# Token rows of u by VectorE block transposes and transfers inside SBUF instead of TensorE transposes, in a fused attention and Fourier-mixing kernel

## The chip, the cores and the metric

The kernel runs on one core of one Trainium2 chip. The metric is the device time of one execution in microseconds (us), the median of several runs. A core has a matrix engine (TensorE, PE), a vector engine (VectorE, DVE), a scalar engine (ScalarE, ACT), GpSimd (POOL) and a queue engine (SyncE, SP) that here only issues transfers (DMAs). Each engine works through its own list of instructions in order; an instruction that waits holds up all that stand behind it on its engine.

## The reference, cut to what matters

Four batches of 768 tokens. Attention with 8 heads of 64 channels gives x (768 tokens by 512 channels) of each batch. Then a Fourier mixing layer and a two-layer perceptron:

```python
X = np.fft.fft(np.fft.fft(x, axis=1), axis=2)
u = x + np.real(X)
mu = np.mean(u, axis=-1, keepdims=True)
var = np.mean((u - mu) ** 2, axis=-1, keepdims=True)
un = (u - mu) / np.sqrt(var + 1e-06)
out = u + np.maximum(un @ w_ch1, 0.0) @ w_ch2     # w_ch1 (512, 2048), w_ch2 (2048, 512)
```

So u is needed twice: with channels on the partitions, as the right operand of the product with w_ch1, and with tokens on the partitions, for the statistics of a token and for the sum with the result.

## The kernel before

All is in fp32. The attention of batch b runs interleaved with the mixing and the perceptron (`mix`, `mlp7`) of batch b-1; those of batch 3 run alone at the end. Within the bulk of the program a scheduler orders the instructions of each engine by its own model of durations, and a tile framework gives out buffers and sets the waits; the code gives the work, not its exact order.

Attention, per pair of heads n and block of keys c (`weigh`, `values`, `scale`): scores (L869), exponentials on ScalarE (L873), a mask by VectorE (L879), VectorE's running sum of the weights (L964), the product with v (L890). When a pair is done its sums are turned and inverted: L908 on TensorE, L915, L917, L918 and L925 on VectorE, eight small copies L924 on ScalarE, and L929 scales x.

`mix` adds the Fourier transform to x in place, in four blocks of 128 channels (matmuls L1091, sums L1105). After it x holds u turned: channel on the partition, token along the row, as x[:, c, token] with c from 0 to 3.

`mlp7` multiplies by blocks in Strassen's manner (Winograd's form): seven products instead of eight. The left operands are blocks of w_ch1 and sums of them (A11, A12, A22, S1 to S4), written to DRAM (`ad`) in batch 0 and fetched from there into a ring of NR = 12 buffers, one for each product (L1339, on SP; a fetch waits until the product that last used its buffer is done). The right operands are the quarters b11, b12, b21, b22 of x and the sums t1, t2, t4 (L1344 to L1346) and t3 (L1351); t3 is written over b12. So whatever reads the first two channel blocks of tokens 384 to 767 must have read them before t3 is written.

For each of 16 row blocks (two halves of eight, index f) the loop `inner` makes seven products of two matmuls of 128x384 each (L1366), in four PSUM banks' worth of names p1, p6, p5, p7, which come from a pool of two banks while attention runs beside it. ScalarE copies each result out of PSUM, which frees the bank, VectorE adds (L1392, L1399, L1404, L1408, L1416) and ScalarE applies relu; four pieces of `hall` result. `outer7` then makes the second layer from `hall`, one half after the other (L1246).

`across(b, T, u)` makes token rows: for one of six blocks T of 128 tokens, four TensorE transposes of 128x128 (L1117) into PSUM and one ScalarE copy of 128x512 into the buffer of T (L1118). For T = 3, 4, 5 it runs before t3 is written, for T = 0, 1, 2 in the first row block of `inner` (in batch 0, after the first half). Four of the six buffers (`us`) lie in the memory of w_ch1, which is free after batch 0; two come from a pool. `spread` takes the statistics of each T from them (L1123, L1125, then POOL) when `outer7` begins on the first half; the last sums add the result to the same rows and `store` sends them out.

The memory of w_ch1 is cut up by hand: the ring, the sums t1, t2, t4, the rows `us`, two side buffers.

Of the kernel before, what the change touches and what calls it, by code (L numbers as in the profile page):

```python
# [11 lines left out]
F32 = mybir.dt.float32  # L12
# [8 lines left out]
P = 128  # L21
B, H, S, D = 4, 8, 768, 64
NBITS = 6
DM = H * D
DFF = 4 * DM
NT = S // P
# [4 lines left out]
NDC = DM // P  # L31
GTT = 2
GT = GTT * P
# [446 lines left out]
def _main(  # L480
# [13 lines left out]
    nc = tc.nc  # L494
# [13 lines left out]
    def wt(shape, dtype, tag, name, bufs=2):  # L508
        return work.tile(shape, dtype, tag=tag, name=name, bufs=bufs)
# [4 lines left out]
    def pt(shape, name):  # L514

        turn[0] += 1
        if roomy[0] and turn[0] % 2:
            if turn[0] % 4 == 1:
                return ps_o.tile(shape, F32, tag="o", name=name)
            return ps_sc.tile(shape, F32, tag="sc", name=name)  # L520
        return ps_1.tile(shape, F32, tag="ps", name=name)
# [468 lines left out]
    GT = NT // 2  # L990
# [54 lines left out]
    def mix(b):  # L1045
# [39 lines left out]
        for j in range(NDC):  # L1085
# [22 lines left out]
            yield  # L1108

        yield from mlp7(b)  # L1110

    def across(b, T, u):

        x = xs[b]
        ps = pt([P, NDC, P], f"un{b}_{T}")
        for c in range(NDC):
            nc.tensor.transpose(ps[:, c, :], x[:, c, T * P : (T + 1) * P], ident)  # L1117
        nc.scalar.copy(u, ps.rearrange("p c n -> p (c n)"))  # L1118

    def spread(b, T, u):  # L1120
# [14 lines left out]
    HF = NFC // 2  # L1135
    A11, A12, A22, S2, S1, S3, S4 = range(7)
    ad = tc.dram_tile([HF, 7, P, 2, P], F32, name="ad")
    w1f = w1.rearrange("p c f -> p (c f)")
    NR = 12
    ring = [  # L1140
        w1f[:, i * 2 * P : (i + 1) * 2 * P].rearrange("p (k m) -> p k m", k=2)
        for i in range(NR)
    ]
    at = NR * 2 * P
    bs = [
# [1 line left out]
        for i in range(3)  # L1147
    ]
    at += 3 * S
    us = [w1f[:, at + i * DM : at + (i + 1) * DM] for i in range(4)]  # L1150
    at += 4 * DM
    side = [w1f[:, at + i * HALF : at + (i + 1) * HALF] for i in range(2)]
    HD = DM // 2
    tq = wt([P, 6, HD], F32, "tq", "tq", 1)
# [154 lines left out]
    def mlp7(b):  # L1309
        x = xs[b]  # L1310
# [5 lines left out]
        ut, sd, ss = [*us], side, s1s  # L1316
        if b == 0:
# [9 lines left out]
            ut = spare[0:3] + [s1s[1].rearrange("p r n -> p (r n)")]  # L1327
# [8 lines left out]
        def fetch():  # L1336
            n = fetched[0]
            if b and n < len(todo):
                nc.sync.dma_start(ring[n % NR], ad[todo[n][0], todo[n][1]])  # L1339
                fetched[0] += 1  # L1340

        for _ in range(NR):
            fetch()
        nc.vector.tensor_tensor(t1, b12, b11, op=ALU.subtract)  # L1344
        nc.vector.tensor_tensor(t2, b22, t1, op=ALU.subtract)
        nc.vector.tensor_tensor(t4, b21, t2, op=ALU.subtract)  # L1346
        ut += [wt([P, DM], F32, "u", f"u{b}_{T}", 2) for T in range(4, NT)]
        for T in (3, 4, 5):
            across(b, T, ut[T])
        rs = {}  # L1350
        nc.vector.tensor_tensor(t3, b22, b12, op=ALU.subtract)  # L1351
        hall = wt([P, 2, HF // 2, S], F32, "F", f"h{b}", 1)
        done = [0]

        def product(i, ps, start=True):
            n = done[0]
            left = ring[n % NR]
            if b == 0:
# [14 lines left out]
        def inner(half):  # L1373
            for r in range(HF // 2):
                f = half * HF // 2 + r
                c11, c12, c21, c22 = (
                    hall[:, i, r, g * HALF : (g + 1) * HALF]
                    for i in range(2) for g in range(2)
                )

                def bank(nm):
                    return pt([P, HALF], f"h{b}_{f}_{nm}")

                p1 = bank("p1")
                product(A11, p1)
                nc.scalar.copy(c12, p1)  # L1388
                p6 = bank("p6")
                product(S2, p6)  # L1390
                nc.scalar.copy(c21, p6)  # L1391
                nc.vector.tensor_tensor(c21, c12, c21, op=ALU.add)  # L1392
                yield
                product(A12, p1, False)
                nc.scalar.activation(c11, p1, AF.Relu)
                p5 = bank("p5")
                product(S1, p5)
                nc.scalar.copy(c22, p5)  # L1398
                nc.vector.tensor_tensor(c22, c21, c22, op=ALU.add)  # L1399
                yield  # L1400
                p7 = bank("p7")
                product(S3, p7)
                nc.scalar.copy(sd[0], p7)  # L1403
                nc.vector.tensor_tensor(c22, c22, sd[0], op=ALU.add)  # L1404
                nc.scalar.activation(c22, c22, AF.Relu)
                product(S4, p5, False)
                nc.scalar.copy(c12, p5)
                nc.vector.tensor_tensor(c12, c21, c12, op=ALU.add)  # L1408
                nc.scalar.activation(c12, c12, AF.Relu)
                if b and f == 0:  # L1410
                    for T in range(3):
                        across(b, T, ut[T])
                yield
                product(A22, p7, False)
                nc.scalar.copy(sd[1], p7)
                nc.vector.tensor_tensor(c21, c21, sd[1], op=ALU.add)  # L1416
                nc.scalar.activation(c21, c21, AF.Relu)
                if b == 0 and r < HF // 2 - 1:
                    quarters(f + 1)
                if r % 2:  # L1420
                    yield
# [148 lines left out]
```

## Time and profile before

| | |
|---|---|
| time, three runs (us) | 1104.84, 1107.59, 1108.07; median 1107.59 |
| the profiled execution (us) | 1106.46; its span from first to last instruction 1104.7 |
| TensorE clock granted | 0.991 of full |
| transfers | 175567 packets, 103.13 MB, mean 93 GB/s |

The profile is one execution, taken by the hardware profiler. A group line gives the source line, the engine, the operation, "output <- inputs" by the program's names, the shapes and the count, then the busy time and the mean of one in ns, then the idle time of that engine just ahead of these instructions and what ended it. The chain of waits goes back from the last instruction, at each step to what released it. A timeline line gives start and length in us; a bracket is the engine's idle time before it and what ended it. Starts of TensorE's matmuls overlap, so the distance between starts is what one costs.

### The profile page before, as it was taken

To read this page: it belongs to the slowest core of one execution; us is meant where nothing else is said; L and a number is where in the kernel's file an instruction comes from. 1 tells how busy PE (TensorE), PEld (TensorE's weight loads), DVE (VectorE), ACT (ScalarE), POOL (GpSimd) and SP (SyncE) were. 2 spreads that over 40 slices of the span, in tenths; PEclk is the share of its full clock that TensorE was granted. 3 is DMA by queue.
4 is the path that set the end of the run, shared out by engine and by line. 5 is a ranking of instruction groups with operands and counts; after the bars stand their busy time and mean duration, and the time that the engine had idled before them with its cause. 6 is when DMAs were issued, how large, how long until landed. Compare 5 with 4: busy or idle time off the path is not lost.

```text
span 1104.7 us, 14065 instructions
## 1 busy us (share of the span) xinstructions
PE 1050.9 (95%) x4893; PEld 636.6 (58%) x4893; DVE 790.0 (72%) x1326; ACT 500.3 (45%) x1055; POOL 63.1 (6%) x141
## 2 busy tenths in 40 slices
PE   6989888999989999999999999999999999999996
PEld 3334354445744675545664576645674569768575
DVE  5779968979598977786758785975856785644353
ACT  5869556654267324354426424354315532340420
POOL 0000000002000020010000011001000002100000
PEclk9989999999999999999999999999999999999998
DMA  8744534261046262313144134213032205122301
GB/s 225 201 99 96 101 106 109 99 196 26 20 130 183 73 192 52 63 58 76 26 152 110 49 67 167 44 38 91 20 109 85 69 26 172 53 82 91 119 20 42
DMA packets 175567, 103.13 MB, mean 93 GB/s; under 512 B 129408, under 2 KB 162816, under 8 KB 175488
## 3 DMA queue, kind: packets, MB, share of 16 engines
q1 hardware_dynamic: 168400, 83.93, 28.8%
q0 software_dynamic: 5520, 17.83, 5.2%
q8 instruction: 41, 0.67, 0.2%
q10 hardware_dynamic: 1568, 0.39, 0.2%
q14 instruction: 38, 0.31, 0.1%
HBM read 81.14 MB, written 20.97 MB: 92 GB/s over the span
## 4 chain that ended last, share of the span: by engine, by line
PE 56%; DVE 8%; ACT 3%; issue 1%; DMA 1%; DVEq 0%; ACTq 0%
PE o L1246 20%; PE h_p L1366 19%; PE oo L890 6%; PE sc L869 5%; PE cs L1062 2%; DVE pk L879 2%; PE A L1091 2%; PE B L1091 1%; DVE acc L964 1%; ACT rr L924 1%; DMA zraw<-in_moe_w_ch_dram 1%; PE un L1117 1%; DVE w L1258 1%; PE bits L804 1%; DVE h L1232 1%
## 5 line engine op out<-in xcount | busy, mean ns | idle before, releaser
L1246 PE MATMUL o<-w,h 128*128 128x256 f32 x1152 | 259.4, 382 | 1.1 <-ACT tq L1265 0.7
L1246 PEld LDWEIGHTS o<-w,h 128*128 128x128 f32 x1152 | 216.3, 190 | 43.5 <-issue 4.6
L873 ACT ACTIVATE pk<-sc 128x768 f32<-128x768 f32 x192 | 148.0, 808 | 82.4 <-PE sc L869 63.9
L1366 PE MATMUL h_p<-x,w 128*128 128x384 f32 x448 | 163.1, 494 | 3.6 <-ACT h L1388 2.3
L890 PE MATMUL oo<-pk,vn 128*64 128x385 f32 (+1 forms) x768 | 156.9, 503 | 3.6 <-DVE pk L879 3.0
L869 PE MATMUL sc<-qt,kt 64*128 64x384 f32 x768 | 155.3, 507 | 3.3 <-ACT pk L873 3.0
L879 DVE SCALAR_TENSOR_TENSOR pk<-qb,kb,pk 128x768 f32<-128x768 bf16 x132 | 128.9, 1012 | 29.1 <-ACT pk L873 28.9
L1366 PEld LDWEIGHTS h_p<-x,w 128*128 128x128 f32 x448 | 82.0, 190 | 71.0 <-ACT pk L873 5.4
L964 DVE TENSOR_TENSOR acc<-acc,pk 128x1536 f32<-128x1536 f32 (+1 forms) x72 | 105.7, 1482 | 6.6 <-ACT pk L873 6.1
L1366 PE MATMUL h_p<-w 128*128 128x384 f32 x288 | 105.5, 489 | 2.2 <-ACT w L1403 2.2
L890 PEld LDWEIGHTS oo<-pk,vn 128*64 128x64 f32 x768 | 49.7, 137 | 98.6 <-issue 71.8
L869 PEld LDWEIGHTS sc<-qt,kt 64*128 64x128 f32 x768 | 67.0, 188 | 48.7 <-issue 24.8
L1366 PEld LDWEIGHTS h_p<-w 128*128 128x128 f32 x288 | 53.7, 190 | 41.7 <-ACT w L1403 3.5
L1276 ACT COPY tq<-o 128x256 f32<-128x256 f32 x24 | 8.9, 373 | 105.2 <-PE o L1246 105.2
L1258 DVE SCALAR_TENSOR_TENSOR w<-o,rs,w 128x256 f32<-128x256 f32 x56 | 26.8, 479 | 41.6 <-PE o L1246 41.6
L1246 PE MATMUL o<-w 128*128 128x256 f32 x176 | 42.3, 383 | 1.4 <-DVE w L1258 1.3
L1392 DVE TENSOR_TENSOR h<-h 128x384 f32<-128x384 f32 x32 | 17.8, 555 | 31.9 <-ACT h L1391 31.8
L1265 ACT COPY tq<-o 128x256 f32<-128x256 f32 x24 | 8.9, 371 | 69.3 <-PE o L1246 69.2
L1000 POOL DMA_DIRECT2D out_dram<-w x30 | 16.3, 546 | 388.7 <-issue 293.2
L1246 PEld LDWEIGHTS o<-w 128*128 128x128 f32 x176 | 32.8, 190 | 8.8 <-DVE w L1258 2.9
L1399 DVE TENSOR_TENSOR h<-h 128x384 f32<-128x384 f32 x32 | 17.7, 553 | 26.8 <-ACT h L1398 26.8
L1292 DVE TENSOR_TENSOR tq<-tq,o 128x256 f32<-128x256 f32 x24 | 10.0, 418 | 34.7 <-PE o L1246 34.7
(170 smaller groups left out, 1350.7 us busy)
## 6 DMA issues: line engine op xcount, KB each, us to landing
w<-ad SPq DMA_DIRECT2D x168, 128.0 KB, 2.0
w<-bd SPq DMA_DIRECT2D x42, 512.0 KB, 4.4
zraw<-in_moe_w_ch_dram POOLq DMA_DIRECT2D x21, 512.0 KB, 4.1
bd<-w SPq DMA_DIRECT2D x14, 512.0 KB, 3.8
vn<-in_v_dram SPq DMA_DIRECT2D x32, 192.0 KB, 3.5
qn<-in_q_dram SPq DMA_DIRECT2D x120, 48.0 KB, 2.4
kn<-in_k_dram SPq DMA_DIRECT2D x60, 96.0 KB, 3.3
ad<-tq SPq DMA_DIRECT2D x8, 512.0 KB, 3.0
```

The lines of the kernel that those rows point to most:

```text
L869: last[0] = nc.tensor.matmul(ps[:, h, 0:HALF], kt[rows, ks], qt[rows, qs], start=kb is not None, stop=True,)
L873: nc.scalar.activation(pk[:, g, :, 0:HALF], ps[:, :, 0:HALF], AF.Exp, scale=SCALE)
L879: nc.vector.scalar_tensor_tensor(w, qb[:, h].rearrange("p (g s) -> p g s", g=2), kb[:, h, c : c + 1], w, op0=ALU.is_equal, op1=ALU.mult,)
L890: nc.tensor.matmul(oos[g][h * D : (h + 1) * D, 0:w], nat["v", n][:, (2 * c + h) * D : (2 * c + h + 1) * D], pk[:, g, h, 0:w], start=(c == ...
L964: nc.vector.tensor_tensor(acc[:, g], (first if c == 1 else acc)[:, g], new[:, g], op=ALU.add,)
L1062: nc.tensor.matmul(ps[:, pc + 2 * lo : pc + 2 * hi - 1 : 2], z[:, cp, pc, par, t * P : (t + 1) * P], ch[:, cp, pc, lo:hi], start=(cp == 0) ...
L1091: nc.tensor.matmul(ps[:, cols], F[:, par, k, t, j * P : (j + 1) * P], sq[:, t, k, cols], start=(t == 0), stop=(t == 1),)
L1246: nc.tensor.matmul(ps, a[:, r], right7[i][:, r], start=start and r == 0, stop=r == HF // 2 - 1, skip_group_check=not start,)
L1258: nc.vector.scalar_tensor_tensor(t[:, cols], src, r, t[:, cols], op0=ALU.mult, op1=ALU.add)
L1366: nc.tensor.matmul(ps, left[:, k], right[i][:, k], start=start and k == 0, stop=k == 1, skip_group_check=not start,)
L1392: nc.vector.tensor_tensor(c21, c12, c21, op=ALU.add)
L1399: nc.vector.tensor_tensor(c22, c21, c22, op=ALU.add)
```

## The change

In batches 1 to 3 `across` is no longer called. Instead VectorE transposes x in 32x32 blocks (`nc.vector.transpose`: each block of 32 partitions by 32 columns is turned in its place): six instructions, for two channel blocks c = 0, 1 of tokens 384 to 767 ahead of t3, then c = 0, 1 of tokens 0 to 383, then c = 2, 3 whole. They write to the second half of the memory of `hall` (row blocks 2 and 3 of four), which is now allocated before t3. Sixteen transfers, issued by SP from SBUF to SBUF, then put the blocks in place: transfer (i, j) takes from the 32 partitions of channel group i the block columns of token group j and writes them to the 32 partitions of token group j. Each moves 32 partitions x 24 x 32 floats. All six row buffers are now in the memory of w_ch1 (`u6`), so that one transfer can reach all of them; the room comes from the ring, NR = 8 instead of 12. The layout of `hall` has its two middle dimensions exchanged, so that row blocks 2 and 3 are contiguous. Batch 0 is as before.

```diff
-    NR = 12
+    NR = 8
...
-    us = [w1f[:, at + i * DM : at + (i + 1) * DM] for i in range(4)]
-    at += 4 * DM
+    u6 = w1f[:, at : at + NT * DM].rearrange("p (t m) -> p t m", m=DM)
+    us = [u6[:, T] for T in range(NT)]
+    at += NT * DM
...
-        ut += [wt([P, DM], F32, "u", f"u{b}_{T}", 2) for T in range(4, NT)]
-        for T in (3, 4, 5):
-            across(b, T, ut[T])
+        hall = wt([P, HF // 2, 2, S], F32, "F", f"h{b}", 1)
+        if b == 0:
+            ut += [wt([P, DM], F32, "u", f"u{b}_{T}", 2) for T in range(4, NT)]
+            for T in (3, 4, 5):
+                across(b, T, ut[T])
+        else:
+            turns = hall[:, 2:4].rearrange("p r i n -> p (r i n)").rearrange(
+                "p (t c n) -> p c t n", c=NDC, n=P
+            )
+            tiles = x.rearrange("p c (t n) -> p c t n", n=P)
+            for c in range(2):
+                nc.vector.transpose(turns[:, c, GT:], tiles[:, c, GT:])
         rs = {}
         nc.vector.tensor_tensor(t3, b22, b12, op=ALU.subtract)
-        hall = wt([P, 2, HF // 2, S], F32, "F", f"h{b}", 1)
+        if b:
+            for c in range(2):
+                nc.vector.transpose(turns[:, c, 0:GT], tiles[:, c, 0:GT])
+            for c in range(2, NDC):
+                nc.vector.transpose(turns[:, c], tiles[:, c])
+            blocks = hall[:, 2:4].rearrange("p r i n -> p (r i n)").rearrange(
+                "p (t j a) -> p j t a", j=4, a=32
+            )
+            to = u6.rearrange("p t (c i a) -> p i (t c) a", i=4, a=32)
+            for i in range(4):
+                for j in range(4):
+                    nc.sync.dma_start(
+                        to[32 * j : 32 * j + 32, i], blocks[32 * i : 32 * i + 32, j]
+                    )
+        hall = hall.rearrange("p r i n -> p i r n")
...
-                if b and f == 0:
-                    for T in range(3):
-                        across(b, T, ut[T])
```

## The prediction

> **What bounds the kernel now.** First the totals of busy time and the chain of work that ended last:
>
> ```profile
> PE 1050.9 (95%) x4893; PEld 636.6 (58%) x4893; DVE 790.0 (72%) x1326; ACT 500.3 (45%) x1055; POOL 63.1 (6%) x141
> PE 56%; DVE 8%; ACT 3%; issue 1%; DMA 1%; DVEq 0%; ACTq 0%
> ```
>
> TensorE is busy in 95% of the span, so at first sight every microsecond taken from it counts. The transposes to be removed are this group:
>
> ```profile
> L1117 PE MATMUL un<-ident,x 128*128 128x128 f32 x96 | 14.2, 280 | 1.1 <-DVE x L1105 1.1
> L1118 ACT COPY w<-un 128x512 f32<-128x512 f32 x16 | 8.9, 586 | 15.5 <-PE un L1117 15.5
> ```
>
> Of 96 transposes 72 go (24 stay in batch 0). The mean of 280 ns overlaps the next one; on the chain of waits twelve in a row take 1.45 us, so one costs 0.121 us of TensorE, 24 cost 2.9 us, 72 cost 8.7 us. But a change in a few places must be read there. Busy time of the engines in stretches (columns: PE, PEld, DVE, ACT, POOL busy us, granted clock, DMA share, GB/s): the second batch's turning point, what follows it, and the last batch's:
>
> ```profile
> 456.00:492.00 36.00, 34.59 (x148) 17.51 (x144) 27.40 (x39) 20.04 (x43) 3.05 (x8) 1.00 0.22 54
> 492.00:716.00 224.00, 221.54 (x1044) 136.92 (x1044) 163.79 (x254) 89.10 (x189) 10.52 (x22) 1.00 0.33 86
> 947.00:975.00 28.00, 27.59 (x101) 16.98 (x100) 14.85 (x30) 14.28 (x31) 5.38 (x12) 1.00 0.29 85
> ```
>
> After 492 TensorE idles 2.5 us in 224: what is won or lost before it is carried to the end. From 456 to 492 it idles 1.4 us and stretches some matmuls (eight of L890 take 2.90 us at 476.60, against 1.44 elsewhere). The chain of waits in that stretch shows who holds it (start us, us, what):
>
> ```profile
> 469.23 1.65 DVE acc L964
> ...
> 473.29 0.98 DVE rt L925
> 474.27 0.44 DVE h L1404
> 474.71 0.87 DVE x L929
> 475.58 0.98 DVE pk L879
> 476.56 0.04 issue
> 476.60 2.90 PE oo L890 x8
> ```
>
> Here the chain runs through VectorE and ScalarE, not TensorE. VectorE's idle time in the same stretch is what could take the added transposes (timeline of DVE; in brackets the idle time before):
>
> ```profile
> 462.29 0.96 DVE L1351 TENSOR_TENSOR x<-x 128x768 f32<-128x768 f32 x1 [2.11 <-PE un L1117]
> ...
> 465.67 0.56 DVE L1392 TENSOR_TENSOR h<-h 128x384 f32<-128x384 f32 x1 [2.42 <-ACT h L1391]
> ...
> 468.18 0.56 DVE L1399 TENSOR_TENSOR h<-h 128x384 f32<-128x384 f32 x1 [1.95 <-ACT h L1398]
> ```
>
> [...]
>
> **The change part by part.**
>
> *Removed, per batch:* 24 transposes, 2.9 us of TensorE; six L1118 copies, 6 x 0.59 = 3.5 us of ScalarE; t3 (L1351) no longer waits for TensorE (4.2 us over the batches).
>
> *Added on VectorE, per batch:* two transposes of 128x768 and four of 128x384. L760 is 0.973 us; neighbours on VectorE start about 0.07 us before the record of the last ends, so 0.90 and 0.46: 2 x 0.90 + 4 x 0.46 = 3.6 us. They stand ahead of the first h sum (L1392).
>
> *Added transfers:* 16 of 32 partitions x 24 x 32 floats, 96 KB in 128-byte pieces: the shape of the k loads, which read DRAM. Their row:
>
> ```profile
> L562 SPq DMA_DIRECT2D kn<-in_k_dram x60: 311/524/2216, 15.2 to 715.5; - x60
> ...
> DMA to landing us min/median/max: 2.3/3.3/6.9
> ```
>
> So SP needs 0.52 us to issue one, and where they follow closely (us 94 to 95) the queues move 155 to 173 GB/s: 98304 B / 165 GB/s = 0.60 us each. Call the price r: 0.52 below (SP's issue), 1.0 above, for a source in SBUF that no row shows; I take 0.60. Sixteen land 16r + 2 = 11.6 us after the start. Behind the waiting first one on SP's queue stand the weight fetches (L1339).
>
> *Ring of 8 for 12:* a product takes 1.29 us, eight 10.3 us; a fetch lands in 2.0 us. Nothing, apart from the fetches queued behind the sixteen. The new layout of h keeps runs of 128 or 384 floats: nothing.
>
> *Moved:* the instruction order of the changed program differs from the old only in about 35 us after each of the three turning points. There the six statistics (L1123) and six aggregates (L1125), 3.6 + 0.9 = 4.5 us, which were spread between other work, stand in one block, because they need all sixteen transfers. Queued behind the block on VectorE are sums of h row block f=1; ScalarE's relu waits for those, behind it the copies that free PSUM, and TensorE for these.
>
> Products are numbered as they are written, seven to each f, from 0 (so 14 is the first of f=2).
>
> *Batches 1 and 2* (equal, 259.4 us apart). x is whole at 456.3. From there VectorE's new order: transposes 3.6, t2, t4, t3 2.7, h sum 0.5, two L879 1.9, h sum 0.5, L915 0.5, L964 1.7, L917, h sum, L918 0.9, wait for ScalarE's relu and eight L924 copies 2.0, L925 0.9, h sum 0.5, L929 0.9, wait for the next exponentials 1.2, L879 1.9, L964 1.7, h sum 0.5, L879 1.9, L964 1.7, L879 1.9, L964 1.7, the block 4.5, two h sums 1.0: 34.5 us, so 490.8. ScalarE's relu and the copy that frees the bank: +1.0, product 14 (f=2) starts at 491.8; before, 492.3. Its bank then takes product 16 after a sum, relu, copy, the k norm (L742, 0.95, moved here) and relu, copy: 495.2, before 494.9. TensorE, which had been some 5 us ahead, has waited from about 487 for it. The transfers, 462.7 + 11.6 = 474.3, are long in. Each batch: +0.3. On ScalarE the removed copies and on TensorE the removed transposes only lengthen waits here. Bounds: -4.4 (2.9 of transposes and 1.4 of idle) if the block does not hold TensorE up, +1.5 if each handover costs 0.1 more.
>
> *Batch 3, alone.* TensorE's new order puts a half of S1's product ahead of S2's, so it no longer waits for t2 and reaches f=1 at 955.8, before 959.2: 3.4 us ahead. VectorE ends the transposes at 954.6, so the transfers start at 954.7 and land at 954.7 + 11.6 = 966.3. Two things wait: fetch 13, issued after the sixteenth (about 963.2 by SP's issue, 964.3 by the queue) and in at about 966, wanted at 963.5; and the statistics, which could start at 964.7. The block ends at 966.3 + 4.5 = 970.8, then sum, relu, copy 1.5: product 16 at 972.3, before 970.8. So +1.5; with r = 0.52 it is +0.2; with 1.0, +7.9.
>
> Sum: 0.3 + 0.3 + 1.5 = +2 us on a span of 1104.7. That execution took 1106.5 us, the three runs 1104.8 to 1108.1, median 1107.6. Forecast 1107.6 + 2 = **1109.6 us**.
>
> **Rivals.** *A, faster:* the block is not where TensorE's time goes, and 2.9 us a batch come out in batches 1 and 2, none in 3 (the block's bound): -5.8, 1101.8; at the most 2 x 4.4 and 3.7 in batch 3, 1095. For it: 95% of TensorE. Against: VectorE's chain above. *B, slower:* the transfers inside SBUF are slower than loads. At r = 1.0 batch 3 loses 7.9 and the whole is +8.5, 1116.1; it passes +3.3 us from r = 0.68. Batches 1 and 2 join only past r = 1.27 ((485 - 462.7 - 2) / 16). For it: both ends lie in 32 partitions and nothing like it is in the trace[...]. *C:* the smaller ring alone starves the products: needs a fetch late by 10.3 us; the longest blocks of SP between fetches of batches 1 to 3 are shorter (4.6 us in the second half of batch 1), so 0.03, folded into B.
>
> **How the numbers follow.** Forecast 0.49, A 0.22, B 0.29. A measurement here can tell about 0.3%, 3.3 us: below 1104.3 is faster, above 1110.9 slower. The forecast's own range is 1106 to 1113 (r 0.52 to 0.75, +0.5 for handovers), of which 0.38 lies within 0.3% and 0.11 above; A gives 0.20 faster and 0.02 same, B 0.27 slower and 0.02 same. Faster 0.20, same 0.42, slower 0.38. The range takes in the middle of A and B's r = 1.0: 1101 to 1117.
>
> **What would show it.** Right: VectorE without a pause from 456 to 490 in batch 1, TensorE idle 4 to 5 us near 487 before a product, the sixteen issued in 8 to 10 us, the statistics in batch 3 waiting for a transfer until about 966. Wrong: statistics' block short or no idle TensorE (A); landing over 1 us apart, TensorE waiting for w (B).

## The result and the profile after

| | before | after |
|---|---|---|
| median (us) | 1106.84 (1104.84 to 1108.07) | 1113.49 (1112.55 to 1114.54) |
| ratio, 95% interval | | 1.0062 [1.0043, 1.0081] |
| span of the profiled execution (us) | 1104.7 | 1112.7 |
| granted clock of TensorE, mean | 0.991 | 0.986 |

The kernel before was run a fourth time here, which moves its median from 1107.59 to 1106.84. The changed kernel is 0.6% slower, 6.9 us by the ratio (4.8 to 9.0). First the totals and the chain of waits on the page of the changed kernel, and the group of TensorE transposes that is left:

```profile
PE 1047.6 (94%) x4821; PEld 631.5 (57%) x4821; DVE 801.3 (72%) x1344; ACT 490.9 (44%) x1037; POOL 62.5 (6%) x141
PE 53%; DVE 17%; ACT 4%; issue 3%; DMA 2%; SPq 1%; POOL 0%; DVEq 0%; ACTq 0%
L1117 PE MATMUL un<-ident,x 128*128 128x128 f32 x24 | 3.7, 283 | 0.7 <-DVE x L1105 0.7
```

Seventy-two transposes are gone, and TensorE has less to do. Yet the chain that sets the end runs through VectorE twice as much as before (17% instead of 8%), and SP's issuing (SPq) has come onto it. The same three stretches as before, of the changed kernel (busy us of PE, PEld, DVE, ACT, POOL; granted clock, DMA share, GB/s):

```profile
456.00:492.00 36.00, 31.70 (x121) 14.89 (x122) 31.64 (x47) 15.81 (x36) 4.89 (x12) 0.97 0.54 103
492.00:716.00 224.00, 221.54 (x1032) 136.83 (x1030) 160.96 (x246) 89.16 (x189) 8.72 (x17) 0.99 0.32 83
947.00:975.00 28.00, 22.98 (x77) 14.13 (x76) 18.25 (x36) 8.41 (x18) 1.54 (x4) 0.94 0.59 117
```

Where 1.4 us of TensorE's time was idle from 456 to 492 it is now 4.3, and in the last batch 5.0 instead of 0.4. The granted clock is below 1.00 in all three, where before it was 1.00. VectorE's timeline in batch 1 of the changed kernel, with the block of statistics (start, length, what; a bracket is idle time before):

```profile
484.50 1.28 DVE L1123 BATCH_NORM_STATS2 bs<-w 128x6 f32<-128x512 f32 x2
...
489.18 0.55 DVE L1426 TENSOR_TENSOR h<-h 128x384 f32<-128x384 f32 x1
```

and TensorE's, for the products behind those sums (four records of 128x384 are one product; these are numbers 13 to 16):

```profile
485.90 1.45 PE L1393 MATMUL h_p<-w 128*128 128x384 f32 x4
491.37 2.93 PE L1393 MATMUL h_p<-x,w 128*128 128x384 f32 x4 [4.01 <-ACT h L1434]
494.09 2.77 PE L1393 MATMUL h_p<-w 128*128 128x384 f32 x4
496.65 1.64 PE L1393 MATMUL h_p<-x,w 128*128 128x384 f32 x4
```

The block stands from 484.50 to 489.18; then sum, relu, a copy that frees PSUM (L1434), and product 14 after 4.01 us of idle TensorE. From product 14 to 15 and from 15 to 16 it takes 2.72 and 2.56 us where 1.29 is normal: half speed. The trace's record of the granted clock says the same. Just before the slow products and during them (columns as above):

```profile
486.77:490.18 3.41, 0.58 (x2) 0.00 (x0) 2.93 (x9) 0.00 (x0) 2.74 (x9) 1.00 0.31 78
490.18:497.01 6.83, 5.64 (x9) 3.19 (x10) 1.32 (x3) 3.62 (x9) 1.43 (x3) 0.50 0.07 19
```

The last batch, SP's, VectorE's and TensorE's lines:

```profile
951.48 5.75 SPq L1340 DMA_DIRECT2D w<-ad  x5
957.71 11.59 SPq L1376 DMA_DIRECT2D w<-h  x16
969.41 15.85 SPq L1340 DMA_DIRECT2D w<-ad  x15
...
971.74 1.29 DVE L1123 BATCH_NORM_STATS2 bs<-w 128x6 f32<-128x512 f32 x2 [3.17 <-DMA w<-ad]
...
972.21 2.90 PE L1393 MATMUL h_p<-w 128*128 128x384 f32 x4 [5.02 <-DMA w<-ad]
974.90 2.77 PE L1393 MATMUL h_p<-x,w 128*128 128x384 f32 x4
977.47 1.87 PE L1393 MATMUL h_p<-w 128*128 128x384 f32 x4
979.17 1.45 PE L1393 MATMUL h_p<-x,w 128*128 128x384 f32 x4
```

SP spends 957.7 to 969.3 on the sixteen, and the fetch that product 13 wants goes out behind them. (The bracket of the statistics names a fetch as well; by the code they need the rows of u, so I take the last of the sixteen, which landed at about that time, to have ended their wait.) The transfers' own row in the last batch:

```profile
L1376 SPq DMA_DIRECT2D w<-h x16: 585/654/807, 957.7 to 968.7; - x16
DMA to landing us min/median/max: 2.5/3.1/3.5
```

**One measure for all that follows.** The same kernel's profiles differ by several us in the start of the program (x of batch 1 is whole at 456.33 us before, at 452.30 in a run whose order of work is the same). What repeats is the distance between two events of one stretch. I use two: in batches 1 and 2, from the end of the last L1105 (x whole) to the first L804 (the next attention's bits), and in batch 3 from x whole to the first product of the second layer. Before, these are 41.24, 41.24 and 38.01 us. In all runs (us; the ratio is to the kernel before, with its 95% interval):

| kernel | batch 1 | batch 2 | batch 3 | ratio |
|---|---|---|---|---|
| before | 41.24 | 41.24 | 38.01 | 1 |
| after | 43.67 | 42.49 | 43.16 | 1.0062 [1.0043, 1.0081] |
| e1_ring8 | 41.24 | 41.23 | 38.01 | 0.9999 [0.9983, 1.0016] |
| e2_only12 | 43.89 | 42.59 | 38.01 | 1.0050 [1.0034, 1.0066] |
| e3_late | 36.94 | 36.94 | 43.00 | 0.9990 [0.9972, 1.0008] |
| e8_before_turn | 44.07 | 44.07 | 38.01 | 1.0055 [1.0033, 1.0077] |
| e6_four | 39.62 | 40.93 | 42.29 | 1.0027 [1.0008, 1.0046] |
| e4_pool3 | 42.58 | 42.44 | 38.80 | 1.0041 [1.0024, 1.0058] |
| e7_inter | 38.25 | 38.24 | 38.07 | 0.9954 [0.9939, 0.9969] |
| e9_late12 | 36.94 | 36.95 | 38.01 | 0.9939 [0.9920, 0.9959] |
| e10_before_late | 41.24 | 41.25 | 38.01 | 1.0008 [0.9994, 1.0023] |
| e11_wide | 37.82 | 37.82 | 41.01 | 0.9963 [0.9946, 0.9981] |
| e12_fill3 | 43.38 | 42.34 | 43.12 | 1.0071 [1.0045, 1.0097] |
| e13_fill6 | 43.84 | 42.58 | 42.00 | 1.0061 [1.0043, 1.0079] |

The change costs 2.4 + 1.3 + 5.2 = 8.8 us by this measure; the spans are 8.0 us apart, the runs 6.9 (4.8 to 9.0).

### The profile page after: what moved, and what is told of

It is laid out like the page before. It is cut to its first block, busy times and chain, and to the rows that moved or that the text cites. A ratio compares the mean times of both kernels' runs of the same rounds, so it can differ in the third digit from the quotient of the medians.

```text
span 1112.7 us, 13967 instructions
## 1 busy us (share of the span) xinstructions
PE 1047.6 (94%) x4821; PEld 631.5 (57%) x4821; DVE 801.3 (72%) x1344; ACT 490.9 (44%) x1037; POOL 62.5 (6%) x141
## 4 chain that ended last, share of the span: by engine, by line
PE 53%; DVE 17%; ACT 4%; issue 3%; DMA 2%; SPq 1%; POOL 0%; DVEq 0%; ACTq 0%
PE o L1247 22%; PE h_p L1393 16%; PE oo L890 5%; PE sc L869 5%; DVE pk L879 4%; DVE acc L964 2%; PE cs L1062 2%; DMA zraw<-in_moe_w_ch_dram 2%; PE A L1091 1%; SPq L1376 1%; ACT rr L924 1%; DVE w L1259 1%; PE B L1091 1%; DVE h L1233 1%; DVE x L1105 1%
## 5 line engine op out<-in xcount | busy, mean ns | idle before, releaser
L1393 PE MATMUL h_p<-x,w 128*128 128x384 f32 x448 | 168.4, 506 | 12.6 <-ACT h L1434 8.0
L890 PE MATMUL oo<-pk,vn 128*64 128x385 f32 (+1 forms) x768 | 155.4, 502 | 2.2 <-DVE pk L879 2.1
L1393 PE MATMUL h_p<-w 128*128 128x384 f32 x288 | 109.1, 503 | 5.0 <-DMA w<-ad 5.0
L890 PEld LDWEIGHTS oo<-pk,vn 128*64 128x64 f32 x768 | 49.3, 136 | 95.8 <-issue 71.5
L1259 DVE SCALAR_TENSOR_TENSOR w<-o,rs,w 128x256 f32<-128x256 f32 x68 | 32.4, 480 | 46.0 <-PE o L1247 45.9
L1000 POOL DMA_DIRECT2D out_dram<-w x42 | 22.6, 541 | 399.6 <-DVE w L1259 397.1
L1247 PE MATMUL o<-w 128*128 128x256 f32 x176 | 42.3, 383 | 1.3 <-DVE w L1259 1.3
L1419 DVE TENSOR_TENSOR h<-h 128x384 f32<-128x384 f32 x32 | 17.7, 552 | 31.0 <-ACT h L1418 30.9
L1062 PE MATMUL cs<-ch,z 128*128 128x128 f32 (+3 forms) x192 | 32.3, 318 | 2.3 <-DVE bt L808 1.3
```

Of the source, the lines that this page charges most:

```text
L890: nc.tensor.matmul(oos[g][h * D : (h + 1) * D, 0:w], nat["v", n][:, (2 * c + h) * D : (2 * c + h + 1) * D], pk[:, g, h, 0:w], start=(c == ...
L1000: (nc.sync if b == B - 1 else nc.gpsimd).dma_start(out[b, s0 : s0 + 2 * w - 1 : 2, cols], src[at : at + w, cols])
L1062: nc.tensor.matmul(ps[:, pc + 2 * lo : pc + 2 * hi - 1 : 2], z[:, cp, pc, par, t * P : (t + 1) * P], ch[:, cp, pc, lo:hi], start=(cp == 0) ...
L1247: nc.tensor.matmul(ps, a[:, r], right7[i][:, r], start=start and r == 0, stop=r == HF // 2 - 1, skip_group_check=not start,)
L1259: nc.vector.scalar_tensor_tensor(t[:, cols], src, r, t[:, cols], op0=ALU.mult, op1=ALU.add)
L1393: nc.tensor.matmul(ps, left[:, k], right[i][:, k], start=start and k == 0, stop=k == 1, skip_group_check=not start,)
```

## The experiments

My theory T, after the result: in batches 1 and 2 the block of statistics holds the sums, TensorE idles 4 us and is then slow; in batch 3 SP's issuing holds up a fetch. Rivals: the ring (R2), VectorE's transposes themselves (R1), the transfers' way through the DMA engines (R3), slow products that have another cause than idle time (R4).

### The ring alone, and one part of the batches alone

e1_ring8, the kernel before with

```diff
-    NR = 12
+    NR = 8
```

> The kernel before with the ring of 8 buffers in place of 12, and nothing else. Theory T (in batches 1 and 2 the six statistics in one block hold the sums, so TensorE idles 4 us and then runs at half clock; in batch 3 the sixteen issues on SP hold up a fetch): the ring takes no part, time within 0.15% of before (ratio 0.9985 to 1.0015), no product waits for a fetch for more than 0.5 us. Rival R2 (the smaller ring alone costs part of the 6 us): ratio 1.002 to 1.006, and products waiting for w from ad in the profile, 1 to 2 us in each of batches 1 to 3.

Measured 0.9999 [0.9983, 1.0016], and all three stretches as before to 0.01 us. The smaller ring alone costs nothing; R2 is out. No run has the sixteen transfers with a ring of 12, so it is not shown that the ring's size plays no part beside them: in batch 3 five fetches go out ahead of the sixteen (951.48), with eight buffers those of products 8 to 12. With twelve, five fetches in that place would be those of products 12 to 16, so product 13 could have its weights ahead of the sixteen.

e2_only12, the change in batches 1 and 2 alone:

```diff
-        if b == 0:
+        if b in (0, B - 1):
...
-        if b:
+        if b in (1, 2):
             for c in range(2):
                 nc.vector.transpose(turns[:, c, 0:GT], tiles[:, c, 0:GT])
...
+                if b == B - 1 and f == 0:
+                    for T in range(3):
+                        across(b, T, ut[T])
```

> The change in batches 1 and 2 alone; batch 3 turns u by TensorE as before. T: batch 3's share, 5.1 us by the events of the two traces, is gone, and the 4.0 us of batches 1 and 2 stay: about 1111 against 1107 before, ratio 1.0035 (1.002 to 1.005); TensorE's idle of 4.0 us ahead of a product and the 2.7 us products after it stay in both batches, and no product waits 5 us for w. If the shares were wrongly read and batch 3 is not more than a third of the loss: ratio 1.005 or more. If batches 1 and 2 only carry a loss that they give back later: ratio within 1.0015.

The stretches are 43.89, 42.59 and 38.01: batch 3 is back to its old length, and batches 1 and 2 keep their loss of 2.7 + 1.4 = 4.0 us (0.36%). The ratio, 1.0050, holds this within its interval, at its lower end; it is at the border of the second expectation too, so here the trace decides, not the ratio. The loss has two places that don't touch each other.

### Taking the block of statistics out of the way

e3_late, the changed kernel with

```diff
-                nc.vector.tensor_tensor(c21, c21, sd[1], op=ALU.add)
+                last_sum = nc.vector.tensor_tensor(c21, c21, sd[1], op=ALU.add)
+                for T in {2: (0, 3), 3: (1, 4, 2, 5)}.get(f, ()) if b else ():
+                    with tc.issue_after(last_sum.ins):
+                        rs[T] = spread(b, T, ut[T])
```

> The changed kernel with the statistics of T = 0 and 3 put behind the last sum of row block f = 2 and the four others behind that of f = 3, in batches 1 to 3, so that no block of them stands ahead of the sums of f = 1. T: the 4.0 us of idle TensorE and the half clock after it (some 3 us in batch 1, 2 us in batch 2) go, product 14 starts within 1 us of the end of product 13; about 6.5 us less in each of batches 1 and 2, batch 3 as in the changed kernel (5 us wait for w): 1113.5 - 13 = 1100.5, ratio 0.994 to before. Rival R4 (the slow products after the idle have another cause than the idle): only 4 us less in each, ratio 0.998. Rival (the statistics hold the later sums as they held these): the idle comes back near f = 3 or at the start of the second layer, ratio 1.004 to 1.006.

TensorE in batch 1 of this run, products 13 to 15:

```profile
487.73 1.45 PE L1393 MATMUL h_p<-w 128*128 128x384 f32 x4
489.02 1.45 PE L1393 MATMUL h_p<-x,w 128*128 128x384 f32 x4
490.31 1.45 PE L1393 MATMUL h_p<-w 128*128 128x384 f32 x4
```

No idle time and no slow product. The stretch falls to 36.94 us, by 6.7 in batch 1 and 5.6 in batch 2, and is now 4.3 us *shorter than before the change*. Two things kept the ratio at 0.9990, above the 0.994 that I expected: from the bits to the next whole x this run takes 219.36 and 192.58 us where the kernel before takes 218.13 and 191.37, so 1.2 us a batch are given back (TensorE idles 1.58 us for VectorE's L915 at 526.95; the likely reason is that four statistics stand behind one sum, ahead of that work on VectorE); and batch 3 keeps its 5.0. Together -4.3 - 4.3 + 1.2 + 1.2 + 5.0 = -1.2 us, which is the ratio. In batch 3 the statistics are out of the way as well, and its stretch is 43.00: there the block alone is not what makes the length.

e6_four leaves four of the six in the block:

```diff
+                if b and f == 1:
+                    for T in (0, 3, 1, 4):
+                        rs[T] = spread(b, T, ut[T])
+                if b and f == 2:
+                    with tc.issue_after(last_sum.ins):
+                        for T in (2, 5):
+                            rs[T] = spread(b, T, ut[T])
```

> The changed kernel with the statistics of T = 2 and 5 put behind the last sum of row block f = 2 in batches 1 to 3: the block ahead of the sums of f = 1 keeps four of six statistics, 3.0 of 4.5 us. By the traces the stretch from x whole to the bits (L804) is 36.9 us without the block and 43.7 (batch 1) and 42.5 (batch 2) with all of it. T (the slow products are the clock's answer to 4 us of idle TensorE, which a shorter idle doesn't call up): idle 2.5 us, the products after it stay 1.29 us apart, the stretch 39.5 us in both batches. Rival R4 (slow products whatever the length of the idle): idle 2.5 us, then products of 2.7 us, the stretch 42 us in batch 1 and 41 in batch 2. Batch 3 not better than in the changed kernel by more than 1.5 us. Ratio 1.000 under T, 1.004 under R4.

Product 14 and what follows it, in batch 1 and in batch 2:

```profile
487.39 1.56 PE L1393 MATMUL h_p<-x,w 128*128 128x384 f32 x4 [2.20 <-ACT h L1434]
488.91 1.56 PE L1393 MATMUL h_p<-w 128*128 128x384 f32 x4
...
745.15 1.57 PE L1393 MATMUL h_p<-x,w 128*128 128x384 f32 x4 [2.20 <-ACT h L1434]
746.67 2.93 PE L1393 MATMUL h_p<-w 128*128 128x384 f32 x4
749.39 1.75 PE L1393 MATMUL h_p<-x,w 128*128 128x384 f32 x4
```

The idle time follows the length of the block, 4.01 to 2.20 us. But the same 2.20 us are followed by no slow product in batch 1 (stretch 39.62, as T expected) and by one of 2.72 us in batch 2 (40.93, as R4 expected). So the length of the idle time alone does not decide.

The traces' record of the clock shows what else does. In the changed kernel the granted clock is at 0.50 in spells that begin at 490.18, 753.01 and 971.46, which lie 77 and 64 steps of 3.413 us apart, and last two steps, one and two. Ahead of each stands a step in which TensorE did little (0.58, 0.00 and 0.00 us of work in 3.41). In e6_four, the step with the idle time in batch 1, then the one in batch 2 and the one after it:

```profile
483.74:487.15 3.41, 1.45 (x5) 0.57 (x3) 2.55 (x7) 0.70 (x2) 2.85 (x7) 1.00 0.42 111
743.15:746.56 3.41, 1.41 (x4) 0.68 (x4) 1.48 (x3) 1.72 (x5) 2.08 (x5) 1.00 0.19 48
746.56:749.98 3.42, 3.42 (x6) 1.85 (x6) 0.74 (x2) 2.02 (x6) 0.00 (x0) 0.50 0.13 38
```

In batch 2 the clock falls at 746.56, when TensorE has been at work again for 1.4 us; that is why product 14 still has full speed there and product 15 has not. From 300 to 1050 us, in all runs, sixteen steps at full clock with at most 1.41 us of work were followed by half clock, and none with 1.45 us or more. Why the border lies there isn't shown; in batch 0 steps with 1.57 us (the kernel before, 60.15 to 63.56) and 1.62 us (e12_fill3, 174.60 to 178.01) were followed by half clock as well. How an idle time falls on these steps is not given by its length, and part of the loss hangs on it: the changed kernel, e2_only12, e4_pool3, e12_fill3 and e13_fill6 all have 4.01 or 4.02 us of idle time in batches 1 and 2, and their stretches are 43.4 to 43.9 us where the low spell has two steps and 42.3 to 42.6 where it has one.

### Is the slow clock the idle time's, or the late weights'?

e12_fill3 and e13_fill6 put matmuls that nobody reads into batch 3's wait, three and six of them:

```diff
+            if b == B - 1 and n == 13:
+                idle = pt([P, HALF], "idle")
+                with tc.issue_after(prev[0].ins):
+                    for k in range(6):
+                        prev[0] = nc.tensor.matmul(
+                            idle, ident, x[:, 3, 0:HALF], start=True, stop=True
+                        )
+                pin = tc.issue_after(prev[0].ins)
```

> The changed kernel with three idle matmuls (identity by x, 128x384, 0.64 us each, into a PSUM buffer that nothing reads) in batch 3 between product 12 and product 13, the one that waits 5.0 us for its fetch. They don't shorten the wait's end, they only fill 1.9 us of it, from 5.0 to 3.1 us of idle TensorE. In the changed kernel the three products after the wait start 2.7, 2.6 and 1.7 us apart instead of 1.29: 3.1 us lost. T (the slow products are the clock's answer to the length of the idle time): idle of 3.1 us lies between 2.2, which called them up in one of two cases, and 4.0, which did so every time, and 3.1 us in the run with POOL's transfers did not; so either no slow product (stretch from x whole to the first product of the second layer 40.1 us) or one (41.5). Rival R4 (the late weights or the full DMA engines slow the products, not the idle): 43.2 us as in the changed kernel.

> The same with six idle matmuls, 3.9 us of the 5.0 us of the wait, so that TensorE is idle for 1.1 us only. T: no slow product at all, product 13 starts where it started (20.7 us after x is whole), the next ones 1.29 us apart, the stretch from x whole to the first product of the second layer 40.1 us instead of 43.2, ratio to before 1.0034 against 1.0062 for the changed kernel. Rival R4: slow products as before, stretch 43.2 us. If the six stand in the way of product 13 (their end after its fetch): up to 1 us more than 40.1.

With three, then with six (TensorE in batch 3; the first line of each is product 13 or the filling):

```profile
970.87 2.90 PE L1404 MATMUL h_p<-w 128*128 128x384 f32 x4 [3.15 <-DMA w<-ad]
```

```profile
971.43 4.03 PE L1398 MATMUL idle<-x,ident 128*128 128x384 f32 x12
976.69 1.53 PE L1404 MATMUL h_p<-w 128*128 128x384 f32 x4 [1.23 <-DMA w<-ad]
978.06 1.45 PE L1404 MATMUL h_p<-x,w 128*128 128x384 f32 x4
979.35 1.45 PE L1404 MATMUL h_p<-w 128*128 128x384 f32 x4
982.31 1.56 PE L1404 MATMUL h_p<-x,w 128*128 128x384 f32 x4 [1.51 <-ACT h L1426]
```

Product 13 starts 20.8 us after x is whole in both, as in the changed kernel (20.7). With 1.23 us idle the products after it are 1.29 to 1.37 us apart, although the weights are as late and the same sixteen transfers go ahead of them; with 3.15 they are slow. That is the idle time's doing, and R4 falls. By itself e12_fill3 came out as R4 had it (43.12 us, three slow products, where T had at most one); it is e13_fill6 that tells the two apart. The gain was not the 3.1 us that I expected, though, but 1.16 (43.16 to 42.00): at full speed TensorE runs into the next wait, 1.51 us ahead of product 16, which the late statistics hold up. The ratio can't tell 1.2 us (1.0061 against 1.0062).

What the traces show of the slow clock is half speed (granted clock 0.50, products 2.7 us apart for 1.29) in spells of one or two steps of 3.41 us, 77 and 64 of which lie between the spells of the changed kernel. The step ahead of one of them held 1.41 us of work (e6_four). Told by idle times, in these stretches of all runs: 1.23 to 1.70 us had no slow products, 2.20 us had one in one case of two, 3.12 us had none (e4_pool3, where it falls on two steps, with 2.22 and 1.48 us of work), 3.15 us had three (e12_fill3, one step with 1.23), and the fourteen from 3.96 to 5.34 us all had them, one to three products each.

### SP's issuing or the transfers' way?

e4_pool3 lets POOL issue the sixteen of batch 3:

```diff
-                    nc.sync.dma_start(
+                    (nc.gpsimd if b == B - 1 else nc.sync).dma_start(
```

> The changed kernel with the sixteen transfers of batch 3 issued by POOL instead of SP. The stretch of batch 3 from x whole to the first product of the second layer is 38.0 us in the kernel before and 43.2 in the changed one. T (SP's time to issue, 0.70 us each, holds fetch 13): SP's fetches go out at once, TensorE's wait of 5 us for w and the slow products after it go; what stays are the statistics, which still wait for the last transfer; if POOL issues one in 0.55 us, as its other transfers, the stretch becomes 36 to 39 us, ratio 1.001; if POOL takes 1 us for each, the statistics come 5 us later, the stretch 40 to 42 us, with TensorE waiting for ScalarE or VectorE and not for w. Rival R3 (the transfers' own way through the DMA engines is what takes 0.7 us each): fetches issued early still land late, a product waits for w for 3 us or more, stretch 42 to 43.5 us.

Batch 3 of this run: the transfers' row and landing, the engines in 4 us (last two numbers: DMA share, which counts a packet where it starts and so can pass 1, and GB/s), and TensorE's one wait:

```profile
L1376 POOL DMA_DIRECT2D w<-h x16: 715/716/759, 955.1 to 966.6; - x16
...
DMA to landing us min/median/max: 3.4/6.4/8.0
```

```profile
964.00:968.00 4.00, 4.00 (x14) 2.29 (x13) 1.27 (x3) 2.30 (x5) 2.87 (x5) 1.00 1.11 161
```

```profile
973.86 0.91 PE L1393 MATMUL h_p<-x,w 128*128 128x384 f32 x2 [3.12 <-DMA w<-ad]
```

The stretch is 38.80: 4.4 of the 5.2 us are back. Not all of that need be the issuing's: in this run VectorE's order in batch 3 changed too, and the last sum of f = 1 (966.62) stands ahead of the statistics (974.12) and not behind them. The fairer partner is e3_late, where the statistics stand behind that sum as well and SP issues: 43.00, so 4.2 us less with POOL. Neither expectation is met whole. SP's fetches now go out in time, as T had it; they land late (up to 8.2 us after issue, 2.9 in the changed kernel), as R3 had it, and a product still waits 3.12 us for one. The DMA engines are full (share 1.11), and the sixteen take 6.4 us to land instead of 3.1. In this run the second issuer took the issuing off SP and left the load on the DMA engines.

e11_wide keeps SP and makes the pieces longer:

```diff
-                "p (t c n) -> p c t n", c=NDC, n=P
+                "p (t j c a) -> p c t j a", c=NDC, j=4, a=32
...
-            to = u6.rearrange("p t (c i a) -> p i (t c) a", i=4, a=32)
+            to = u6.rearrange("p t (i w) -> p i t w", i=4)
```

> The changed kernel with the transfers' pieces four times as long: VectorE's transposes write the four channel blocks of a token group next to each other, and each of the sixteen transfers moves the same 96 KB in 192 pieces of 512 bytes instead of 768 of 128. The rows of u then hold their channels in another order, so the sums with the result are not the reference's; the amount of work is the same. Read in batch 3. If the price of a transfer is by the piece: SP issues one in 0.30 to 0.47 us, the sixteen are out in 5 to 8 us instead of 11.6, the DMA engines are less than 80% busy meanwhile unless they move more than 190 GB/s, TensorE's wait of 5 us for w goes or falls under 2 us without slow products after it, and the stretch from x whole to the first product of the second layer is 37 to 40 us instead of 43.2. If the price is by the byte (SBUF as source and target limits to 140 GB/s): 0.65 to 0.72 us each, engines 95% busy, the stretch 42.5 to 43.5 us. In batches 1 and 2 the statistics can stand elsewhere, since they are ordered by modelled durations: no expectation there.

```profile
L1376 SPq DMA_DIRECT2D w<-h x16: 585/606/651, 946.1 to 956.4; - x16
```

```profile
952.00:956.00 4.00, 3.54 (x11) 1.73 (x10) 1.12 (x2) 1.71 (x5) 0.00 (x0) 1.00 0.70 137
```

```profile
959.50 2.75 PE L1393 MATMUL h_p<-w 128*128 128x384 f32 x4 [3.96 <-DMA w<-ad]
```

(The transfers' row, the engines during them, and the wait, all in batch 3.) The engines in the changed kernel:

```profile
964.00:968.00 4.00, 3.19 (x10) 1.52 (x8) 1.12 (x2) 1.84 (x4) 0.00 (x0) 1.00 0.95 140
```

With a quarter of the pieces the DMA engines are only 70% busy (95% in the changed kernel), but SP takes 0.61 us to issue one instead of 0.65, so the sixteen still occupy SP for 11.0 us (11.6 in the changed kernel) and the fetch is still late. So issuing on SP sets the pace, and it is hardly by the piece; the load on the engines is. At 140 GB/s, with the engines 95% busy, 98304 B take 0.70 us (an estimate from these two numbers), and SP starts a transfer each 0.73 us: the two prices are close, which is why each of the two cures alone (e4, e11) uncovers or leaves the other. The shorter stretches of this run in batches 1 and 2 (37.82) say nothing of the pieces: there the scheduler has split the block of statistics. Why SP needs 0.61 us for these and 0.32 us for a fetch of 128 KB is open.

e7_inter spreads the sixteen between the fetches, two behind each of products 0 to 7 in the order of the program, with the statistics late:

```diff
+            for i, j in [moves.pop(0) for _ in range(2)] if b and moves else ():
+                nc.sync.dma_start(
+                    to[32 * j : 32 * j + 32, i], blocks[32 * i : 32 * i + 32, j]
+                )
```

> The changed kernel with two of the sixteen transfers issued behind the fetch of each of the products 0 to 7, in batches 1 to 3, and the statistics of T = 0, 3 behind the last sum of f = 1, of T = 1, 4 behind that of f = 2 and of T = 2, 5 behind that of f = 3. T: both causes are gone: no block ahead of the sums of f = 1, no fetch behind all sixteen. Batches 1 and 2 from x whole to the bits 37 us (before 41.2), at most 1 us of it given back later; batch 3 to the first product of the second layer 35 to 37 us (before 38.0: 2.9 us less on TensorE, up to 1 us more in handovers). Together 8 to 10 us under the kernel before, ratio 0.992. If the transfers hinder the fetches by their use of the DMA engines wherever they stand (R3): batch 3 above 40 us, ratio 0.996 to 0.999.

0.9954, better than before but not the 0.992 expected; batch 3 isn't above 40 us either, as R3 had it. In batch 3, 38.07 us: TensorE has lost its transposes and waits three times for weights instead:

```profile
959.09 1.53 PE L1389 MATMUL h_p<-w 128*128 128x384 f32 x4 [1.01 <-DMA w<-ad]
960.94 1.56 PE L1389 MATMUL h_p<-x,w 128*128 128x384 f32 x4 [0.32 <-DMA w<-ad]
...
964.90 1.53 PE L1389 MATMUL h_p<-x,w 128*128 128x384 f32 x4 [0.74 <-DMA w<-ad]
```

That is 2.1 of the 2.9 us. The transfers were spread less than planned: in the order that the scheduler gave SP, ten still go out in one burst and only six stand between fetches:

```profile
948.60 6.98 SPq L1396 DMA_DIRECT2D w<-h  x10
```

Transfers and fetches together keep SP at work from 948.60 to 961.87, and the fetches among them come late. A full spreading was not tried.

### What the turning itself is worth

e8_before_turn adds VectorE's six transposes to the kernel before; e10_before_late only moves its statistics, with the edit of e3_late and {1: (0, 3), 2: (1, 4), 3: (2, 5)}:

```diff
+            for c in range(2):
+                nc.vector.transpose(turns[:, c, GT:], tiles[:, c, GT:])
         nc.vector.tensor_tensor(t3, b22, b12, op=ALU.subtract)
+        if b:
+            for c in range(2):
+                nc.vector.transpose(turns[:, c, 0:GT], tiles[:, c, 0:GT])
+            for c in range(2, NDC):
+                nc.vector.transpose(turns[:, c], tiles[:, c])
```

> The kernel before with the six VectorE transposes added in batches 1 to 3 at the places that they have in the changed kernel; what they write is not read (TensorE's transposes still make the rows). T: the 3.6 us of VectorE in each batch fall largely into its waits: 0 to 1.5 us per batch, ratio 1.000 to 1.004. Rival R1 (the transposes themselves, standing ahead of the sums on an engine that holds the path there, make the loss): 2.5 to 3.6 us per batch, ratio 1.007 to 1.010.

> The kernel before, u turned by TensorE as ever, with the statistics alone moved: those of T = 0, 3 behind the last sum of f = 1, of T = 1, 4 behind that of f = 2, of T = 2, 5 behind that of f = 3, in batches 1 to 3. It tells how much of the 4.3 us that batches 1 and 2 each win with turning by VectorE and late statistics is the late statistics' own. If the turning brings them (TensorE's 2.9 us and ScalarE's copies taken away): the stretch from x whole to the bits 40.5 to 41.3 us as before (41.2), ratio 0.999 to 1.001. If the statistics bring them (VectorE holds the path there, and they stood in it): the stretch 37 to 38.5 us, ratio 0.993 to 0.996; then turning by VectorE adds next to nothing. Batch 3, where TensorE is busy throughout, as before at 38.0 us either way.

The transposes alone cost 2.83 us in each of batches 1 and 2, more than T expected and what R1 expected there, and nothing in batch 3, which neither had. In batch 1 TensorE waits for the attention's mask, which stands behind them on VectorE:

```profile
459.65 2.44 PE L890 MATMUL oo<-pk,vn 128*64 128x385 f32 x8 [1.69 <-DVE pk L879]
```

In the changed kernel TensorE's order has this L890 at 471.08, behind eight products, and it starts without a wait. So R1 is right for VectorE's transposes beside TensorE's, not for the change. The late statistics alone win nothing (41.24 and 41.25, ratio 1.0008; 0.44 us are lost after each, 218.58 and 191.81 us from the bits to the next whole x). What makes the 4.3 us is therefore the turning, once the block is gone.

### The version that beats both

e9_late12 takes the change in batches 1 and 2 only (e2_only12) and puts the statistics there behind f = 1, 2 and 3, as above.

> The change in batches 1 and 2 alone, with the statistics there put behind the sums of f = 1, 2 and 3 as in the run with interleaved transfers, the sixteen transfers in one go as in the changed kernel; batch 3 turns u by TensorE as before. T: batches 1 and 2 from x whole to the bits 37 us, 4.3 less than before in each, batch 3 38.0 as before: 8.6 us less, at most 1 us given back in each, ratio 0.993. If the statistics hold the sums wherever they stand, the stretch or the one after it is 3 us longer in each batch: ratio 0.998 to 1.000.

1100.62 us (1097.33 to 1100.78), ratio 0.9939 [0.9920, 0.9959]. Stretches 36.94, 36.95, 38.01, and 0.44 us given back after each of the first two (the same 218.58 and 191.81 us as with late statistics alone): -7.7 us, against -6.8 by the ratio (-8.9 to -4.5).

## Why the prediction was right or wrong

**The verdict.** Forecast +2 us, no measurable change; measured +6.9 (4.8 to 9.0), slower by more than 0.3%. The time lies in the range of 1101 to 1117, just past the forecast's own 1106 to 1113; the likeliest case did not come. Of the signs named ahead, TensorE's idle time near 487 and the waiting statistics of batch 3 were seen, but the sixteen took 11.6 us to issue and not 8 to 10, and TensorE waited for w, which was the sign of B.

**The order of VectorE in batches 1 and 2: right.** Product 14 was to come 35.5 us after x is whole (491.8 from 456.3), 36.0 before; it came after 35.54, 35.98 before, in batch 2 after 35.54 as well. TensorE idle for 4 to 5 us from about 487: 4.01 us, until 491.4. The block of 4.5 us was where I put it.

**What follows product 14: the step that failed.** Product 16 was to come after 38.9 us (495.2) and came after 40.8, in batch 2 after 39.8. My sum carried TensorE's idle time as waiting, at the full clock afterwards. It left out the slow clock: after each idle time of 3.96 to 5.34 us in these stretches one to three products ran at half speed (granted clock 0.50). Over the predicted +0.3 that is 2.1 us in batch 1 and 0.9 in batch 2 (2.43 and 1.25 less 0.3), and 1.2 in batch 3 (e13_fill6): 4.2 us that the sum did not have. The wait itself was priced rightly: batch 1 of e6_four, at full clock throughout, takes 5.90 us from product 14 to the bits; after 35.54 that gives 41.44, +0.2 where I had +0.3. By this estimate (the block is shorter in that run) the slow clock is 2.2 us in batch 1 and 1.1 in batch 2. Batch 1 lost more: its low clock lasted two steps of 3.41 us, that of batch 2 one. In the stretches that I read, the idle times of the kernel before were too short to show it (1.12 us at the most from 456 to 492), but its trace has it elsewhere: from 179.59 to 183.01 TensorE is busy 1.36 of 3.42 us, and from 183.01 to 186.42 the granted clock is 0.50.

**The transfers' price: a term that was mis-sized.** I took r = 0.60 us, from 165 GB/s of loads (the kernel before has 158 to 172 GB/s from us 93.00 to 94.25, not from 94 to 95), with 0.52 as the price of issuing, and landing 2 us after the last. Measured: 0.65 us to issue and 0.73 us from start to start (957.7 to 968.7 for fifteen steps), landing after 3.1. The sixteen were in 14.0 us after the start (971.74 - 957.71) instead of 11.6. With that, my own step for batch 3, +1.5 us for product 16, becomes 1.5 + 2.4 = +3.9. Without the slow clock, e13_fill6 has product 16 at 26.42 us after x is whole, the kernel before at 22.53: +3.9. So the path that I had (sixteen transfers, then the statistics, then product 16) is there, with a wrong size, and with the slow clock out of the way it sets product 16. In the changed kernel as it is it doesn't: product 16 follows product 15 without a wait, behind the late product 13 and its slow followers, 27.7 us after x is whole. At full clock that second path would give 20.7 + 3 x 1.29 = 24.6 us, less than the 26.4 of mine (an estimate from the trace); the slow clock makes it the longer one. So with the statistics out of the way (e3_late) batch 3 is as long, 43.00. The landing of 2 us was that of the weight fetches; the row of the k loads in the prediction already had a median of 3.3. Fetch 13 was to be in at about 966, 2.5 us late for TensorE; it came 5.0 us late, by the same issuing. That it would land behind the sixteen in the queue (the 964.3) was my estimate; the trace shows that it was issued behind them (969.41).

**The sum, corrected.** Predicted 0.3 + 0.3 + 1.5 = 2.1; the clock adds 4.2, the transfers 2.4: 8.7 of the 8.8 us by the stretches. So close a sum is no proof of its parts: those of the clock in batches 1 and 2 are what was left over, and in batch 3 two paths overlap.

**Rival A** (2.9 us of transposes and 1.4 of idle, -4.4 a batch, if the block does not hold TensorE up) was the right size for the case that did not occur: with the block out of the way the stretch is 4.3 us shorter (e3_late, e9_late12). **Rival B** was half right: transfers inside SBUF are slower than I took them (0.73 us for 0.60) and TensorE waits for weights in batch 3. But the price is SP's issuing, just ahead of the DMA engines (95% busy, 140 GB/s); 0.73 us from start to start lies past the 0.68 at which B had it become measurable. That small pieces inside SBUF have no price of their own, which my lower price of 0.52 took for granted, was an estimate that no run had shown, and it does not hold here: 128-byte pieces kept the engines 95% busy at 140 GB/s, pieces of 512 bytes 70% busy at 137. Whether it matters that both ends lie in 32 partitions, no run shows. **Rival C**, the ring, costs nothing alone (e1_ring8).

**What hides an edit.** I priced VectorE's six transposes at 3.6 us by L760, the attention's own transpose of 128x768 on VectorE (0.973 us in the kernel before; those of 128x768 in the changed kernel took 0.937), and took them as lying in its idle time, save in the chain to the block. In the order of the changed kernel that was so; e8_before_turn shows that it depends on the order: in the old one they stand ahead of a mask and cost 2.8 us.

## What to carry to other kernels

In the stretches read here each of the fourteen idle times of 3.96 us or more on TensorE was followed by slow products, and one of 2.20 and one of 3.15 us were too. Such an idle time has to be priced with the products after it: removing what held TensorE up here was worth more than the wait itself (4.0 us of waiting, 5.6 to 6.7 us won in e3_late). Filling the wait with idle work won 1.2 us only, since the next wait stood right behind. When a change makes several small instructions ready at one moment, look at where they then stand as one block, and pin them behind work that nobody waits for: here this alone took the loss of 0.6% away (e3_late), and with the last batch left as it was it made a gain of 0.6% (e9_late12). A burst of transfers on a queue that also feeds TensorE is to be counted by issuing time and by the load of the DMA engines, both (here 0.65 us each on SP, and engines 95% busy); curing one alone left or uncovered the other (e11_wide, e4_pool3).

## What was not expected of the hardware

- The granted clock fell to 0.50 for whole steps of 3.41 us, in the changed kernel 2.8 us after the idle time of batch 1 began (487.36, 490.18), in e6_four 3.6 us after that of batch 2 did (742.95, 746.56), when TensorE was back at work: product 14 at full speed, product 15 at half. From 300 to 1050 us of all runs, at most 1.41 us of work in a step brought it each time; told by idle times, 2.20 us did it once and 3.12 us did not.
- A transfer of 96 KB inside SBUF takes SP 0.61 us to issue in 192 pieces and 0.65 us in 768; POOL needs 0.72 us for the latter, where its other transfers take 0.54. The number of pieces hardly shows in the issuing, but it does in the engines' load (70% and 95%).
- Beside the fetches, the same transfers issued by POOL land after 6.4 us (median) instead of 3.1, with the DMA engines' share at 1.11 (us 964 to 968).
